# Sliding-window attention with a SwiGLU block: another order of attention among the feed-forward steps, turned q and k evicted from two banks, and another opening order

## The chip, the cores and the metric

The kernel runs on one core of a Trainium2 chip. The metric is the device time of one execution in microseconds (us). The kernel before has a median of 349.18 us over three runs (349.02 to 349.81). The profile is of one execution of its own. Matrix products run on TensorE (PE), which writes into PSUM, a memory of eight banks. VectorE (DVE) and ScalarE (ACT) read PSUM. GpSimd (POOL) works between tiles in SBUF. SyncE (SP) issues all DMA transfers in one queue.

## The reference

Attention has batch 8, 8 heads, 576 positions and head size 64. Each query sees itself and the 63 keys before it. The result is laid out as 4608 tokens of 512 values, and goes through a gated feed-forward block.

```python
scores = np.matmul(q, k.transpose(0, 1, 3, 2)) / np.sqrt(64)
mask = (rel >= 0) & (rel < 64)            # rel: query position minus key position
attn = softmax(np.where(mask, scores, -1e9))
x = np.matmul(attn, v).transpose(0, 2, 1, 3).reshape(4608, 512)
g = x @ w_gate                            # 512 x 1536
out = (g / (1 + np.exp(-g)) * (x @ w_val)) @ w_out    # w_out: 1536 x 512
```

## The kernel before, in words

Tokens are handled in three sizes. A *group* g is 128 tokens (36 of them), a *block* n is 256 tokens (18), and a *tile* t is 512 tokens (9). The weights stay in SBUF as bf16 after a load and a cast in six slices of 256 columns each (`weights`, `cast_w`; `weights_o`, `casts_o` for w_out). Step m of a tile uses slice m // 2 of both w_gate and w_val.

The attention part of a block loads q and k as f32 (`load`, `load1`, lines 77 to 93) and casts them to bf16 (`cast_k`). It then turns them so that the head dimension lies on the partitions. `turn2` (line 134) does this with eight TensorE transposes into one PSUM bank and copies that evict it. `turn1` (line 126) does it with transposing DMAs. v is loaded and cast per group, into one copy aligned with the group (`vo`) and one shifted by 64 tokens (`ve`).

For a group, `scores` (line 166) makes 16 small matmuls into two banks. `weigh` (line 180) takes the exponential on ScalarE and multiplies by the mask on VectorE (tile `E`, line 189). `products` (line 195) makes 16 small matmuls with v, whose last column of ones sums the weights, into two banks. `norm` (line 209) takes the reciprocal and multiplies, on VectorE, twice each. `turn_x` turns the result on TensorE and evicts it on ScalarE, while `turn_x1` (line 230) turns it by DMA, as in nearly all of the loop. Both write the tile's `xT`.

The feed-forward part of a tile has 12 steps. `step(t, m)` (line 260) makes four matmuls of 512 columns for g, four for v, and the tanh on ScalarE. It is put on a list. `finish()` (line 275) takes the oldest step from that list and does its two VectorE instructions, `sg` (line 278) and `hT` (line 279), which free the step's two banks. A step may cover a part of the 512 columns. `project(t, s)` (line 281) makes 12 matmuls for 128 tokens of a tile, an eviction on ScalarE and the output DMA.

PSUM is cut in two pools. Pool `ps_a` has four banks, given out in turn to turns, scores, products, projects and warm-up matmuls. Pool `ps_f` has two banks for g and two for v.

The order of the program is the order on every engine and in SP's queue. Nothing rearranges it; an instruction waits for its inputs and for its bank or buffer. The opening is a list written out by hand (lines 320 to 562). It runs attention for the first groups with `warm` matmuls (of zeros, line 293) in between, and then the 24 steps of tiles 0 and 1 and the four projects of tile 0, among the attention of groups up to 11. The loop (line 565) then takes one group number w at a time, from 8 to 35. It makes three steps of tile w // 4 and one project of the tile before. In an even w it makes the scores of groups w + 4 and w + 5, and in the odd one after it their products. Six steps and two projects with this attention work are called a *pair* below, and its steps the first to the sixth. In the kernel before, each finish comes one step after its step, and a project follows the third and the sixth step.

Of the kernel before, what the change touches and what calls it, by code (L numbers as in the profile page):

```python
# [8 lines left out]
P = 128  # L9
# [8 lines left out]
def kernel(  # L18
# [58 lines left out]
    def load(n, src, nm):  # L77

        x_f = stage.tile([P, H, 2, D], FP32, name=nm, tag=nm)
        for r, m, b, s, t in segments(256 * n, 256, 2):  # L80
            sp.dma_start(
                x_f[r:r + m].rearrange("r h c d -> r h (c d)"),
                src[b, :, s:s + t, :].rearrange("h (r c) d -> r h (c d)", c=2),
            )
        staged[nm, n] = x_f[:].rearrange("r h c d -> r c h d")
# [19 lines left out]
    def copy(eng, y, x):  # L105
        if eng is act:
            act.copy(y, x)  # L107
        else:
            eng.tensor_copy(y, x)  # L109
# [24 lines left out]
    def turn2(n, nm, eng):  # L134

        x_b = words.pop((nm, n))
        tp = ps_a.tile([P, 4, 2, P], BF16, name="tp", tag="a")
        for c in range(2):
            for p in range(4):
                nc.tensor.transpose(tp[:, p, c], x_b[:, c, P * p:P * p + P], identb[:])  # L140
        o = 64 if nm == "k_f" else 0
        ring = kT[n % KR] if nm == "k_f" else qT[n % QR]
        y = ring[:, :, o:o + 256].rearrange("r p (x c) -> r p x c", c=2)
        x = tp[:].rearrange("r p c x -> r p x c")
        if isinstance(eng, tuple):
            for i in range(2):
                copy(eng[i], y[:, 2 * i:2 * i + 2], x[:, 2 * i:2 * i + 2])
        else:
            copy(eng, y, x)

    def cast_v(g, engs):

# [100 lines left out]
    def casts_o(s, eng):  # L253
        copy(eng, wo[:, 2 * s:2 * s + 2, :], raw.pop((2, s))[:])
# [36 lines left out]
        sp.dma_start(out[n0:n0 + P, :], os_[:])  # L291

    def warm(n):
        w_ps = ps_a.tile([P, 512], FP32, name="w_ps", tag="a")
        for _ in range(n):
            nc.tensor.matmul(w_ps[:], wz[:, 0:P], wz[:])

# [20 lines left out]
            dve.memset(masks[i][0:64, i - 1, :], 0.0)  # L318

    begin()  # L320
    load(1, k, "k_f")
    load(0, q, "q_f")
    load(0, k, "k_f")
    load(1, q, "q_f")
    cast_k(0, "k_f", (act, pool))
    cast_k(0, "q_f", dve)
    warm(11)
    turn2(0, "q_f", (dve, act))
    load_vg(0)
    cast_v(0, pool)  # L330
    load_vg(2)
    cast_v(2, pool)
    cast_k(1, "k_f", (dve, act))
    warm(3)
    turn2(0, "k_f", (dve, act))
    load_vg(1)
    cast_k(1, "q_f", dve)
    turn2(1, "k_f", (dve, act))
    keys_before(1)
    warm(1)  # L340
    turn2(1, "q_f", (dve, act))
    scores(1)
    weigh(1)
    load(2, q, "q_f")
    warm(1)
    scores(0)
    weigh(0)
    warm(1)
    scores(2)
    weigh(2)  # L350
    cast_v(1, pool)
    cast_k(2, "q_f", (dve, act))
    load(3, k, "k_f")
    warm(5)
    products(0)
    norm(0)
    load(2, k, "k_f")
    scores(3)
    weigh(3)
    cast_k(3, "k_f", act)  # L360
    warm(2)
    turn2(2, "q_f", act)
    products(1)
    norm(1)
    turn_x(0)
    load_vg(3)
    cast_k(2, "k_f", (dve, pool))
    load(3, q, "q_f")
    warm(2)
    products(2)  # L370
    norm(2)
    warm(1)
    turn2(2, "k_f", dve)
    turn2(3, "k_f", act)
    weights(0, 1)
    weights(0, 0)
    cast_v(3, pool)
    load_vg(4)
    weights(3, 0)
    turn_x(1)  # L380
    cast_w(0, 0, pool)
    keys_before(3)
    weights(3, 1)
    load_vg(5)
    cast_k(3, "q_f", dve)
    warm(1)
    products(3)
    norm(3)
    keys_before(2)
    turn_x(2)  # L390
    cast_w(0, 1, dve)
    load_vg(6)
    turn2(3, "q_f", (dve, act))
    weights(4, 0)
    warm(1)
    turn_x(3)
    scores(5)
    weigh(5)
    scores(4)
    weigh(4)  # L400
    scores(6)
    weigh(6)
    cast_v(4, pool)
    weights(4, 1)
    cast_w(3, 0, pool)
    step(0, 1)
    step(0, 0)
    finish()
    load_vg(7)
    weights(5, 0)  # L410
    cast_w(3, 1, act)
    products(4)
    norm(4)
    step(0, 7)
    finish()
    weights(5, 1)
    weights(2, 0)
    cast_v(5, pool)
    cast_w(4, 0, pool)
    cast_v(6, act)  # L420
    turn_x(4)
    cast_w(4, 1, pool)
    products(5)
    norm(5)
    weights(2, 1)
    step(0, 6)
    finish()
    products(6)
    norm(6)
    scores(7)  # L430
    weigh(7)
    load_vg(8)
    step(0, 9)
    finish()
    turn_x(5)
    weights(1, 1)
    cast_v(7, pool)
    weights(1, 0)
    turn_x(6)
    cast_w(5, 1, pool)  # L440
    cast_w(5, 0, act)
    load_vg(9)
    load(4, k, "k_f")
    load(5, k, "k_f")
    step(0, 8)
    finish()
    products(7)
    norm(7)
    step(0, 11)
    finish()  # L450
    turn_x(7)
    load(5, q, "q_f")
    step(0, 10)
    finish()
    cast_w(2, 1, dve)
    cast_w(2, 0, act)
    step(1, 8)
    finish()
    load(4, q, "q_f")
    weights_o(2)  # L460
    step(0, 5)
    finish()
    step(0, 4, 0, 256)
    finish()
    load_vg(10)
    weights_o(1)
    cast_w(1, 0, dve)
    step(1, 7)
    finish()
    cast_v(9, pool)  # L470
    weights_o(3)
    cast_w(1, 1, dve)
    step(1, 4)
    finish()
    load_vg(11)
    keys_before(4)
    cast_k(4, "k_f", pool)
    step(1, 11)
    finish()
    step(1, 2)  # L480
    finish()
    cast_k(5, "k_f", (dve, pool))
    turn2(4, "k_f", act)
    weights_o(4)
    weights_o(5)
    step(0, 3)
    finish()
    step(1, 9)
    finish()
    cast_k(4, "q_f", (dve, pool))  # L490
    weights_o(0)
    casts_o(2, pool)
    cast_k(5, "q_f", (dve, pool))
    load1(6, k, "k_f")
    step(0, 2)
    finish()
    cast_v(8, pool)
    turn2(4, "q_f", (dve, act))
    step(0, 4, 256, 256)
    finish()  # L500
    scores(8)
    weigh(8)
    scores(9)
    weigh(9)
    step(1, 5)
    finish()
    products(8)
    norm(8)
    turn2(5, "q_f", act)
    keys_before(5)  # L510
    turn2(5, "k_f", act)
    load1(6, q, "q_f")
    step(1, 1)
    finish()
    products(9)
    norm(9)
    turn_x(8)
    casts_o(3, pool)
    step(1, 0)
    finish()  # L520
    casts_o(1, act)
    casts_o(5, dve)
    casts_o(4, dve)
    cast_k(6, "k_f", dve)
    casts_o(0, act)
    cast_v(11, pool)
    cast_v(10, dve)
    keys_before(6)
    cast_k(6, "q_f", (dve, pool))
    load(7, k, "k_f")  # L530
    scores(10)
    weigh(10)
    turn1(6, "k_f")
    turn1(6, "q_f")
    load_vg(12)
    scores(11)
    weigh(11)
    step(1, 10)
    finish()
    project(0, 3)  # L540
    project(0, 2)
    products(10)
    norm(10)
    turn_x1(9)
    project(0, 1)
    products(11)
    norm(11)
    load_vg(13)
    load1(8, k, "k_f")
    step(1, 3)  # L550
    finish()
    cast_k(7, "k_f", dve)
    step(1, 6)
    finish()
    turn_x(10)
    turn_x(11)
    load1(7, q, "q_f")
    load_vg(14)
    turn2(7, "k_f", dve)
    cast_v(12, pool)  # L560
    keys_before(7)
    project(0, 0)


    for w in range(8, NG):
        t, s = divmod(w, 4)
        n, odd = w // 2, w % 2
        step(t, 3 * s)
        finish()
        if odd:  # L570
            for g in (w + 3, w + 4):
                if g < NG:
                    products(g)
        if odd and n + 4 < NB:
            cast_k(n + 4, "k_f", pool)
        if not odd and n + 3 < NB:
            cast_k(n + 3, "q_f", pool)
        if w + 5 < NG:
            cast_v(w + 5, pool)
        step(t, 3 * s + 1)  # L580
        finish()
        if odd:
            for g in (w + 3, w + 4):
                if g < NG:
                    norm(g)
                    turn_x1(g)
        if not odd and w + 5 < NG:
            scores(w + 4)
            scores(w + 5)
            weigh(w + 4)  # L590
        step(t, 3 * s + 2)
        finish()
        if not odd and w + 5 < NG:
            weigh(w + 5)
        if odd and n + 4 < NB:
            turn1(n + 4, "k_f")
            keys_before(n + 4)
        if not odd and n + 3 < NB:
            turn1(n + 3, "q_f")
        project(t - 1, s)  # L600
        if odd and n + 5 < NB:
            load1(n + 5, k, "k_f")
        if w + 7 < NG:
            load_vg(w + 7)
        if not odd and n + 4 < NB:
            load1(n + 4, q, "q_f")
    finish()
    for s in range(4):
        project(8, s)
# [32 lines left out]
```

## Time and profile before

| what | value |
|---|---|
| median of three runs | 349.18 us |
| the profiled execution | 349.27 us |
| its span, first to last instruction | 347.6 us |
| TensorE busy | 330.8 us, 95% of the span |
| VectorE busy | 239.0 us, 69% |
| ScalarE busy | 146.9 us, 42% |
| GpSimd busy | 99.9 us, 29% |
| DMA queue, share of 16 engines | 76.2%, 56.51 MB |
| chain that ended last | PE 76%, DVE 11%, DMA 7%, issue 2%, ACT 2% |
| mean granted TensorE clock | 0.989 |

The profile's page counts busy time by engine, then cuts the span in 40 slices and gives the busy share of each in tenths. The chain is the work that ended last, followed back from the end: at each step to what released an instruction, or to the instruction before it on its engine. The lists of groups and waits name an instruction by line, engine and tile. "A <- B" in a wait says that A's engine stood idle until B was done. Matmuls overlap in the pipeline, so that four of 512 columns take 0.86 us from start to start of the next four, though each is shown as longer.

### The profile page before, as it was taken

How to read it: one execution, taken by the hardware profiler on the slowest of the kernel's cores; microseconds unless marked ns; L12 is line 12 of the kernel's file. 1: busy time of each engine (PE TensorE's matmuls, PEld its weight loads, DVE VectorE, ACT ScalarE, POOL GpSimd, SP SyncE). 2: the span in 40 equal slices, each digit the busy share in tenths (PEclk: the TensorE clock that was granted, in tenths of full speed). 3: DMA queues.
4: the chain of work that ended last, by engine and by line, in shares of the span. 5: the costliest groups of instructions: out<-in, count | busy, mean ns of one | idle time of the engine just before them, and what ended most of it. 6: DMA issues, size and time to landing. Idle time of an engine off the chain costs nothing.

```text
span 347.6 us, 6974 instructions
## 1 busy us (share of the span) xinstructions
PE 330.8 (95%) x2633; PEld 159.2 (46%) x2633; DVE 239.0 (69%) x500; ACT 146.9 (42%) x252; POOL 99.9 (29%) x145
## 2 busy tenths in 40 slices
PE   6787999999999999999999999989999999999995
PEld 2554444554544444444444444434444444444442
DVE  3788999998869676766676677667766666655510
ACT  1756763484352525252525252525252525223221
POOL 1635704710254242323323332324243220000000
PEclk9889999999999999999999999999999999999999
DMA  8999999995978989979798888988889331210012
GB/s 216 242 281 250 335 260 246 321 209 68 234 145 166 168 179 156 181 168 168 162 162 188 156 167 157 192 146 159 168 180 170 93 91 39 70 46 32 30 62 91
DMA packets 150834, 56.96 MB, mean 164 GB/s; under 512 B 125200, under 2 KB 144656, under 8 KB 150800
## 3 DMA queue, kind: packets, MB, share of 16 engines
q1 hardware_dynamic: 150800, 56.51, 76.2%
q8 instruction: 21, 0.34, 0.4%
q14 instruction: 13, 0.11, 0.1%
HBM read 37.75 MB, written 9.44 MB: 136 GB/s over the span
## 4 chain that ended last, share of the span: by engine, by line
PE 76%; DVE 11%; DMA 7%; issue 2%; ACT 2%; SPq 0%; DVEq 0%; ACTq 0%
PE o_ps L284 24%; PE g_ps L267 23%; PE v_ps L267 22%; DMA xT<-x_b 4%; DVE x_b L214 3%; DVE E L189 3%; PE ao_ps L203 2%; PE s_ps L174 2%; DMA k_f<-in_k_dram 2%; DVE sg L278 2%; PE tp L140 1%; DVE hT L279 1%; DVE r L213 1%; DVE q_fb L109 1%; DMA out_dram<-os__2927 1%
## 5 line engine op out<-in xcount | busy, mean ns | idle before, releaser
L267 PE MATMUL g_ps<-xT,wg 128*128 128x512 bf16 (+1 forms) x436 | 111.4, 378 | 4.2 <-DMA xT<-x_b 2.9
L267 PE MATMUL v_ps<-xT,wv 128*128 128x512 bf16 (+1 forms) x436 | 111.0, 377 | 0.0
L278 DVE SCALAR_TENSOR_TENSOR sg<-th,g_ps 128x512 f32<-128x512 f32 (+1 forms) x109 | 73.8, 677 | 47.5 <-ACT th L272 47.5
L272 ACT ACTIVATE th<-g_ps 128x512 f32<-128x512 f32 (+1 forms) x109 | 64.8, 595 | 86.3 <-PE g_ps L267 80.7
L284 PE MATMUL o_ps<-wo,hT 128*128 128x512 bf16 x432 | 98.3, 379 | 0.0
L279 DVE TENSOR_TENSOR hT<-sg,v_ps 128x512 bf16<-128x512 f32 (+1 forms) x109 | 74.4, 683 | 11.4 <-PE ao_ps L203 0.5
L267 PEld LDWEIGHTS <-wv 128*128 128x128 bf16 x436 | 42.7, 98 | 50.7
L284 PEld LDWEIGHTS <-hT 128*128 128x128 bf16 x432 | 42.2, 98 | 50.5
L267 PEld LDWEIGHTS <-wg 128*128 128x128 bf16 x436 | 39.4, 98 | 48.9 <-DMA xT<-x_b 4.2
L189 DVE TENSOR_TENSOR E<-E,mask 128x512 bf16<-128x512 bf16 x72 | 37.2, 550 | 21.2 <-ACT E L188 20.5
L109 POOL CAST ve<-v_f 64x512 bf16<-64x512 f32 x68 | 42.7, 628 | 4.2
L188 ACT ACTIVATE E<-s_ps 128x512 bf16<-128x512 f32 x72 | 38.4, 604 | 8.9 <-PE s_ps L174 8.7
L109 POOL CAST q_fb<-q_f 128x1024 bf16<-128x1024 f32 (+1 forms) x14 | 13.3, 952 | 77.6 <-DMA q_f<-in_q_dram 63.1
L109 POOL CAST vo<-v_f 128x512 bf16<-128x512 f32 x34 | 22.5, 663 | 36.7 <-DMA v_f<-in_v_dram 36.4
L214 DVE TENSOR_TENSOR x_b<-ao_ps,r 128x256 bf16<-128x256 f32 x72 | 30.6, 425 | 2.5
L109 POOL CAST k_fb<-k_f 128x1024 bf16<-128x1024 f32 (+1 forms) x14 | 13.8, 989 | 58.4 <-DMA k_f<-in_k_dram 53.9
L203 PEld LDWEIGHTS <-E 128*64 128x64 bf16 x576 | 11.5, 111 | 10.8 <-ACT th L272 5.5
L174 PE MATMUL s_ps<-qT,kT 64*128 64x64 bf16 x576 | 13.0, 191 | 3.0 <-ACT qT L107 2.2
L203 PE MATMUL ao_ps<-ve,E 128*64 128x65 bf16 x288 | 14.4, 197 | 0.9 <-DVE E L189 0.5
L213 DVE RECIPROCAL r<-ao_ps 128x4 f32<-128x4 f32 x72 | 12.5, 174 | 3.8 <-PE ao_ps L203 3.7
L174 PEld LDWEIGHTS <-kT 64*128 64x128 bf16 x576 | 10.2, 95 | 10.3 <-issue 8.8
L203 PE MATMUL ao_ps<-vo,E 128*64 128x65 bf16 x288 | 14.4, 198 | 0.0
(84 smaller groups left out, 121.8 us busy)
## 6 DMA issues: line engine op xcount, KB each, us to landing
v_f<-in_v_dram SPq DMA_DIRECT2D x32, 256.0 KB, 4.7
q_f<-in_q_dram SPq DMA_DIRECT2D x23, 256.0 KB, 5.2
k_f<-in_k_dram SPq DMA_DIRECT2D x21, 256.0 KB, 4.1
w_f<-in_moe_w_val_dram SPq DMA_DIRECT2D x6, 512.0 KB, 8.0
w_f<-in_moe_w_gate_dram SPq DMA_DIRECT2D x6, 512.0 KB, 7.7
wo_f<-in_moe_w_out_dram SPq DMA_DIRECT2D x6, 512.0 KB, 8.0
k_f<-in_k_dram SPq DMA_DIRECT2D x5, 512.0 KB, 6.5
q_f<-in_q_dram SPq DMA_DIRECT2D x4, 512.0 KB, 7.8
```

The lines of the kernel that those rows point to most:

```text
L109: eng.tensor_copy(y, x)
L174: nc.tensor.matmul(ps[a][:, p, b], kT[g // 2 % KR][y, p, o:o + P], qT[g // 2 % QR][y, p, o:o + 64], tile_position=(64 * a, 0),)
L188: act.activation(e, x[:], AF.Exp, scale=0.125)
L189: dve.tensor_mul(e, e, mk[:].unsqueeze(1).to_broadcast([P, 4, 2, 64]))
L203: nc.tensor.matmul(o_ps[64 * b:64 * b + 64, i, :], Es[g % ER][:, y, b], z[g % VR][:, y, :], tile_position=(0, 64 * b),)
L213: dve.reciprocal(r[:], o_ps[:, :, D])
L214: dve.tensor_mul(xb[g][:, 256 * h:256 * h + 256].rearrange("r (y d) -> r y d", y=4), o_ps[:, :, 0:D], r[:].unsqueeze(2).to_broadcast([P, 4 ...
L267: nc.tensor.matmul(ps[:, 0:n], w[:, c, P * m:P * m + P], xT[t][:, c, c0:c0 + n], start=(c == 0), stop=(c == 3),)
L272: act.activation(th[:, 0:n], g_ps[:, 0:n], AF.Tanh, scale=0.5)
L278: dve.scalar_tensor_tensor(sg[:, 0:n], th[:, 0:n], 1.0, g_ps[:, 0:n], ALU.add, ALU.mult)
L279: dve.tensor_mul(hT[t][:, m, c0:c0 + n], sg[:, 0:n], v_ps[:, 0:n])
L284: nc.tensor.matmul(o_ps[:], hT[t][:, c, P * s:P * s + P], wo[:, c, :], start=(c == 0), stop=(c == 11),)
```

## The change

There are four parts.

- `turn2` with two engines makes two tiles in two banks, each of half the rows, with all transposes ahead of the two copies. Before, both copies read one bank.
- `warm` takes its bank from the feed-forward pool.
- The opening list is in another order. It begins with k and q of block 0 and ends with turns of block 6 on TensorE, where the list before turned block 6 by DMA and k of block 7 on TensorE. Other engines do some of the casts. The first steps use weight slice 3, then 2, 1, 5, 4 and 0. The step that is cut is (1,7), in three parts (256, 128 and 128 columns) in place of (0,4) in two. The four projects come in the order 1, 0, 3, 2.
- The loop handles two groups at once, with the same steps and projects. The scores come after the first step of a pair, and the first project lies between the second and the third. The products come after the third step, and the second project between the fifth and the sixth. Each finish but the sixth's is put before the next step, some of them behind other work.

The diff follows. In the opening, removed lines are left out, as they are printed above.

```diff
@@ -134,19 +134,21 @@
     def turn2(n, nm, eng):
 
         x_b = words.pop((nm, n))
-        tp = ps_a.tile([P, 4, 2, P], BF16, name="tp", tag="a")
-        for c in range(2):
-            for p in range(4):
-                nc.tensor.transpose(tp[:, p, c], x_b[:, c, P * p:P * p + P], identb[:])
         o = 64 if nm == "k_f" else 0
         ring = kT[n % KR] if nm == "k_f" else qT[n % QR]
-        y = ring[:, :, o:o + 256].rearrange("r p (x c) -> r p x c", c=2)
-        x = tp[:].rearrange("r p c x -> r p x c")
-        if isinstance(eng, tuple):
-            for i in range(2):
-                copy(eng[i], y[:, 2 * i:2 * i + 2], x[:, 2 * i:2 * i + 2])
-        else:
-            copy(eng, y, x)
+        engs = eng if isinstance(eng, tuple) else (eng,)
+        m = 4 // len(engs)
+        tps = []
+        for i in range(len(engs)):
+            tp = ps_a.tile([P, m, 2, P], BF16, name="tp", tag="a")
+            for c in range(2):
+                for p in range(m):
+                    a = P * (m * i + p)
+                    nc.tensor.transpose(tp[:, p, c], x_b[:, c, a:a + P], identb[:])
+            tps.append(tp)
+        for i, tp in enumerate(tps):
+            y = ring[:, m * i:m * i + m, o:o + 256].rearrange("r p (x c) -> r p x c", c=2)
+            copy(engs[i], y, tp[:].rearrange("r p c x -> r p x c"))
 
     def cast_v(g, engs):
 
@@ -291,7 +293,7 @@
         sp.dma_start(out[n0:n0 + P, :], os_[:])
 
     def warm(n):
-        w_ps = ps_a.tile([P, 512], FP32, name="w_ps", tag="a")
+        w_ps = ps_f.tile([P, 512], FP32, name="w_ps", tag="g")
         for _ in range(n):
             nc.tensor.matmul(w_ps[:], wz[:, 0:P], wz[:])
 
@@ -318,292 +320,305 @@
...
             dve.memset(masks[i][0:64, i - 1, :], 0.0)
     begin()
+    load(0, k, "k_f")
+    load(0, q, "q_f")
+    cast_k(0, "k_f", (dve, act))
+    cast_k(0, "q_f", (act, pool))
+    warm(11)
+    turn2(0, "k_f", act)
+    load_vg(0)
     load(1, k, "k_f")
+    warm(3)
+    turn2(0, "q_f", dve)
+    warm(4)
+    scores(0)
+    cast_v(0, (pool, act, dve))
+    cast_k(1, "k_f", pool)
     load(1, q, "q_f")
+    scores(1)
     load_vg(2)
+    load(2, k, "k_f")
+    keys_before(1)
+    weigh(0)
+    cast_k(1, "q_f", dve)
+    weigh(1)
+    warm(2)
+    turn2(1, "k_f", act)
+    warm(2)
+    turn2(1, "q_f", (dve, act))
     load_vg(1)
     load(2, q, "q_f")
     products(0)
     norm(0)
     scores(3)
+    cast_k(2, "k_f", (dve, pool))
     weigh(3)
+    warm(1)
+    turn_x(0)
+    scores(2)
+    cast_v(1, (pool, None, None))
+    weigh(2)
+    load_vg(3)
+    turn2(2, "k_f", act)
+    load(3, k, "k_f")
+    cast_k(2, "q_f", (act, pool))
+    cast_v(2, (pool, dve, act))
+    cast_v(3, (act, pool, pool))
     warm(2)
     products(1)
     norm(1)
+    keys_before(2)
+    warm(4)
+    turn2(2, "q_f", (dve, act))
+    products(2)
     load(3, q, "q_f")
+    warm(1)
+    scores(5)
+    load_vg(4)
     norm(2)
     products(3)
     norm(3)
+    cast_k(3, "k_f", pool)
+    weigh(5)
+    turn_x(1)
+    scores(4)
+    weights(3, 0)
+    cast_k(3, "q_f", pool)
+    weigh(4)
     turn_x(2)
+    cast_v(4, (pool, None, None))
+    cast_w(3, 0, pool)
+    turn2(3, "k_f", act)
+    turn_x(3)
+    keys_before(3)
     warm(1)
+    turn2(3, "q_f", (act, dve))
+    weights(3, 1)
+    warm(2)
     products(4)
     norm(4)
+    cast_w(3, 1, dve)
+    scores(6)
+    load_vg(5)
+    weigh(6)
+    weights(2, 0)
     step(0, 7)
+    cast_v(5, (act, pool, pool))
+    scores(7)
+    finish()
+    weights(2, 1)
+    weigh(7)
+    cast_w(2, 0, act)
+    cast_w(2, 1, pool)
+    load_vg(6)
+    products(5)
+    load_vg(7)
+    step(0, 6)
+    turn_x(4)
+    norm(5)
+    cast_v(6, (act, pool, pool))
+    finish()
+    step(0, 5)
+    turn_x(5)
+    finish()
+    weights(1, 0)
+    cast_v(7, (pool, pool, act))
+    weights(1, 1)
+    cast_w(1, 0, pool)
+    products(6)
+    step(0, 4)
+    weights(5, 0)
     weights(5, 1)
+    products(7)
+    cast_w(1, 1, pool)
+    cast_w(5, 0, pool)
+    step(1, 7, 0, 256)
+    norm(6)
+    weights(4, 1)
+    load(4, q, "q_f")
+    finish()
+    turn_x(6)
+    weights(4, 0)
+    load(4, k, "k_f")
+    load(5, q, "q_f")
+    weights_o(1)
+    load_vg(8)
+    step(0, 3)
+    finish()
+    cast_w(5, 1, pool)
+    norm(7)
+    step(0, 2)
+    finish()
+    finish()
+    turn_x(7)
+    step(0, 10)
+    load_vg(9)
+    step(1, 10)
+    finish()
+    cast_k(4, "q_f", pool)
+    step(0, 11)
+    load(5, k, "k_f")
     cast_w(4, 1, pool)
+    cast_k(4, "k_f", pool)
+    cast_w(4, 0, act)
+    finish()
+    weights(0, 0)
+    load_vg(10)
+    keys_before(4)
+    weights(0, 1)
+    finish()
+    weights_o(0)
+    step(1, 2)
+    finish()
+    step(1, 9)
+    finish()
+    turn2(4, "q_f", (act, dve))
     step(0, 9)
+    turn2(4, "k_f", act)
+    casts_o(1, pool)
+    step(1, 6)
+    finish()
+    finish()
+    weights_o(3)
+    step(1, 7, 256, 128)
+    finish()
+    cast_k(5, "q_f", pool)
+    scores(9)
+    scores(8)
+    cast_v(8, (act, pool, pool))
+    weigh(9)
+    cast_w(0, 0, pool)
+    weights_o(2)
+    weights_o(5)
+    step(1, 11)
+    keys_before(5)
+    cast_k(5, "k_f", act)
     step(0, 8)
+    cast_v(9, (pool, dve, act))
+    finish()
+    finish()
+    weights_o(4)
+    cast_w(0, 1, pool)
+    load_vg(11)
+    weigh(8)
+    step(1, 3)
+    turn2(5, "q_f", act)
     step(1, 8)
+    products(8)
+    finish()
+    products(9)
+    finish()
+    norm(8)
+    step(0, 0)
+    casts_o(0, pool)
+    finish()
+    step(1, 1)
+    turn2(5, "k_f", act)
+    casts_o(3, pool)
+    norm(9)
+    load(6, k, "k_f")
+    turn_x(8)
+    load(6, q, "q_f")
+    step(0, 1)
+    finish()
+    scores(10)
+    cast_v(10, pool)
+    scores(11)
+    finish()
+    weigh(10)
+    load1(7, k, "k_f")
+    casts_o(5, pool)
+    casts_o(2, pool)
+    step(1, 0)
+    weigh(11)
+    casts_o(4, pool)
+    project(0, 1)
+    load_vg(12)
+    cast_v(11, (dve, None, None))
     step(1, 4)
     products(10)
+    cast_k(6, "q_f", pool)
+    finish()
+    cast_k(6, "k_f", (act, pool))
+    products(11)
+    turn_x1(9)
+    step(1, 7, 384, 128)
     norm(10)
+    project(0, 0)
     norm(11)
+    finish()
     load1(7, q, "q_f")
     load_vg(14)
+    turn2(6, "k_f", dve)
+    load1(8, k, "k_f")
+    load_vg(13)
+    project(0, 3)
+    step(1, 5)
+    keys_before(6)
+    turn_x(10)
     keys_before(7)
-    for w in range(8, NG):
+    turn2(6, "q_f", dve)
+    cast_k(7, "k_f", (dve, pool))
+    turn1(7, "k_f")
+    turn_x(11)
+    finish()
+    project(0, 2)
+    cast_v(12, (dve, act, act))
+    for w in range(8, NG, 2):
         t, s = divmod(w, 4)
-        n, odd = w // 2, w % 2
+        n = w // 2
         step(t, 3 * s)
         finish()
-        if odd:
-            for g in (w + 3, w + 4):
-                if g < NG:
-                    products(g)
-        if odd and n + 4 < NB:
-            cast_k(n + 4, "k_f", pool)
-        if not odd and n + 3 < NB:
+        if n + 3 < NB:
             cast_k(n + 3, "q_f", pool)
         if w + 5 < NG:
             cast_v(w + 5, pool)
+            scores(w + 4)
+            scores(w + 5)
+        finish()
+        if w + 5 < NG:
+            weigh(w + 4)
+        step(t, 3 * s + 1)
+        if w + 5 < NG:
+            weigh(w + 5)
+        finish()
+        if n + 3 < NB:
+            turn1(n + 3, "q_f")
+        project(t - 1, s)
+        if w + 7 < NG:
+            load_vg(w + 7)
+        if n + 4 < NB:
+            load1(n + 4, q, "q_f")
+        step(t, 3 * s + 2)
+        w, s = w + 1, s + 1
+        if w + 4 < NG:
+            products(w + 3)
+            products(w + 4)
+        finish()
+        step(t, 3 * s)
+        if w + 4 < NG:
+            for g in (w + 3, w + 4):
+                norm(g)
+                turn_x1(g)
+        if n + 4 < NB:
+            cast_k(n + 4, "k_f", pool)
+        if w + 5 < NG:
+            cast_v(w + 5, pool)
+        finish()
         step(t, 3 * s + 1)
         finish()
-        if odd:
-            for g in (w + 3, w + 4):
-                if g < NG:
-                    norm(g)
-                    turn_x1(g)
-        if not odd and w + 5 < NG:
-            scores(w + 4)
-            scores(w + 5)
-            weigh(w + 4)
-        step(t, 3 * s + 2)
-        finish()
-        if not odd and w + 5 < NG:
-            weigh(w + 5)
-        if odd and n + 4 < NB:
+        if n + 4 < NB:
             turn1(n + 4, "k_f")
             keys_before(n + 4)
-        if not odd and n + 3 < NB:
-            turn1(n + 3, "q_f")
         project(t - 1, s)
-        if odd and n + 5 < NB:
+        if n + 5 < NB:
             load1(n + 5, k, "k_f")
         if w + 7 < NG:
             load_vg(w + 7)
-        if not odd and n + 4 < NB:
-            load1(n + 4, q, "q_f")
+        step(t, 3 * s + 2)
     finish()
     for s in range(4):
         project(8, s)
```

## The prediction, made before the changed kernel had run

> **What bounds the kernel now.** I read the busy rows by slice first, then a table by stage, then the chain that ended last, then the waits of TensorE in the loop. The profiled execution took 349.27 us, of which 347.6 us is the span. The page's slices (40 of 8.7 us):
>
> ```profile
> PE   6787999999999999999999999989999999999995
> DVE  3788999998869676766676677667766666655510
> PEclk9889999999999999999999999999999999999999
> ```
>
> TensorE is full from slice 5 on, with small dents; VectorE is full in slices 4 to 8. The table by stage, cut where the stages change:
>
> ```profile
> 6.70:20.00 13.30, 9.44 (x125) 5.97 (x126) 10.14 (x20) 8.59 (x16) 6.43 (x10) 0.85 1.27 248
> 20.00:31.60 11.60, 8.96 (x152) 5.94 (x150) 8.33 (x23) 6.40 (x12) 5.28 (x8) 0.88 1.17 288
> 31.60:44.10 12.50, 11.28 (x121) 5.76 (x118) 12.09 (x27) 9.87 (x19) 8.58 (x11) 1.00 1.04 301
> 44.10:95.10 51.00, 50.61 (x409) 25.79 (x409) 45.72 (x91) 26.12 (x43) 13.73 (x19) 1.00 0.95 222
> 95.10:347.60 252.50, 245.79 (x1825) 114.25 (x1822) 160.77 (x323) 94.61 (x165) 64.63 (x90) 1.00 0.67 134
> ```
>
> Columns are PE, PEld, DVE, ACT, POOL busy, clock, DMA share, GB/s. The first feed-forward step starts at 31.57. From there to 44.1 VectorE is busy 12.09 of 12.50 us; from 44.1 to 95.1, where the loop starts, TensorE lacks 0.4 us. The chain confirms who rules the opening:
>
> ```profile
> 30.74 4.08 DVE E L189 x6
> 34.82 0.61 DVE sg L278
> ...
> 42.14 1.29 DVE E L189 x2
> 43.44 0.61 DVE sg L278
> 44.04 0.04 issue
> 44.09 1.02 PE g_ps L267 x4
> ```
>
> VectorE's queue carries the end until 44.09, when step (0,8) gets its bank; TensorE carries it afterwards. In the loop TensorE waits for one thing only (waits, then its timeline at the worst place):
>
> ```profile
> PE g_ps L267 <- DMA xT<-x_b: 2.9, 4, 1.2
> ```
> ```profile
> 227.60 1.03 PE L267 MATMUL g_ps<-xT,wg 128*128 128x512 bf16 x4
> 228.47 1.03 PE L267 MATMUL v_ps<-xT,wv 128*128 128x512 bf16 x4
> 229.33 2.75 PE L284 MATMUL o_ps<-wo,hT 128*128 128x512 bf16 x12
> 233.25 1.02 PE L267 MATMUL g_ps<-xT,wg 128*128 128x512 bf16 x4 [1.17 <-DMA xT<-x_b]
> ```
>
> A project keeps TensorE for 2.59 us, so the step should start near 231.9 and starts at 233.25. From one even project to the next the chain gives 16.97 us where nothing waits (100.97, 117.94, 134.90) and 17.53, 17.65, 18.29, 17.97 around the four waits: 0.56 + 0.68 + 1.32 + 1.00 = 3.56 us. A step costs 1.73 us (g 0.865, v 0.865).
>
> **The change, part by part.**
>
> *Loop.* A project now lies between steps, products come before the pair's fourth step instead of after it, and a sixth step follows the odd project. From products to the first step of the next tile stood 2 steps + a project = 6.05 us; now 3 steps + a project, 7.78 us: 1.73 us more for norm, transposing DMA and landing. What starts them doesn't move: in both, one step and the products lie between the end of the even project and norm, the output write and loads of v and q stand ahead of the transposes in SP's queue, and norm waits for one finish. So the landings should keep their distance from the project. In the wait at 163.38 that is 163.25 - 154.47 = 8.8 us, needed at 10.15 now; at the worst place 0.4 us stays. Gain 3.56 us, between 2.5 (landing a us later) and 3.56.
>
> What waits newly here: finish of the fourth step stands behind two norms (2.27 us from 157.39 to 159.66). They begin about 1.5 us after the third step, so that finish ends at 1.5 + 2.27 + 1.4 = 5.2 us; the sixth step, which takes its banks, starts at 0.64 + 1.73 + 1.73 + 2.59 = 6.7. Price 0, with 1.5 us of cover. Scores ahead of the second step put two exponentials (1.2 us) in front of its tanh on ScalarE; its finish is needed after a project and a step, 4.3 us later. Price 0. The last finish, which project (7,3) used to cover, has 11 matmuls of project (8,0), 2.38 us, against about 1.5: 0, at most 0.3.
>
> *Split evictions.* Before, two engines took halves of one bank, and ScalarE's half waited for VectorE's (ACT qT <- DVE qT 4.2 us in 3 waits). In the changed order ScalarE's half waits for TensorE alone. That saves up to 0.7 us of latency on each split turn; it takes no work from VectorE (0.69 us a half), so I count it only in the walk below. The second bank of the four is paid by later tiles; warm gives its bank back, as it now uses a feed-forward one.
>
> *Opening.* First the loads. In the opening DMA is never idle, and landings follow bytes: k 0 (1.57 MB issued by then) at 8.48, k 2 (4.46 MB) at 20.64, gate block 0 (6.29 MB) at 28.39. That is 2.0 us + bytes / 0.24 MB/us. Two weight blocks by the waits at 37.58 and 41.78 (9.17 and 10.5 MB) give 0.315 afterwards. In the new order: k 0 at 4.2, q 0 6.4, k 1 9.6, q 1 11.8, k 2 15.1, q 2 18.4, k 3 21.7, q 3 23.8, v 4 24.9, blocks 3 (6.55 MB) between 28.2 and 29.2, blocks 2 at 32 to 34, blocks 1 at 37 to 39, blocks 5 at 41 to 43.
>
> Then the engines in their new order. q 2 at 18.4, its cast, 8 transposes and two evictions end at 21.9; scores (5) follow, and from there VectorE's queue has no gap that I find. Its work after 21.9: norm 2 and 3 (2.27, and 0.4 waiting for products 3), weigh 5 and 4 (2.56, at 0.64 an E), the small v copies and keys 0.63, half a q turn 0.69, norm 4 1.13, the cast of value block 3 0.69, weigh 6 1.28: 31.6. That cast waits for the load, with weigh 6 and the first finish behind it; VectorE arrives at 29.5, the block by 29.2, so nothing is added if the rate holds, and each us of lateness beyond is a us of everything. The first step runs at 29.4 to 31.1. Then finish 1.37, weigh 7 1.28, norm 5 1.13, two finishes 2.75, norm 6 1.13, finish 1.37, the part step 0.83, norm 7 1.13, two finishes 2.75: 45.3. TensorE follows it, waiting for banks twice, and at 45.4 has done 7.5 steps, products up to 7 and turn_x up to 7. The kernel before has 6 steps and products 7 at 46.28. The difference: 0.88 + 1.5 x 1.73 + 0.24 for the turn = 3.7 us.
>
> Here a rule speaks against the change, since it leaves more casts to GpSimd beside VectorE's weighing. The row: E takes 412 ns at least, 780 at the median before 44.1 (up to 1251), 424 at the median in the loop. The Trainium skill (SBUF — State Buffer, "Who interferes with whom") says that a VectorE instruction with two SBUF inputs contends with a GpSimd one that reads SBUF, and that the later one is blocked whole. By it each E meeting a 1.04 us cast could wait for half of it, about 0.95 us each, an estimate; the 8 E of my sum would be 2.5 us later. In the chain, 14 E take 9.01 us, 0.64 each, beside 11.7 us of GpSimd work from 6.7 to 31.6; the new order has 9.9 before the first step. I take 0.64 and keep 2.5 for the range.
>
> What takes some back: six turns on TensorE after the first step instead of five (0.45 us; in return two fewer transposing DMAs on SP), the third part of the cut step 0.1. Handing-over: the chain up to 46 us has 2.8% "issue", 1.3 us, and my walk has none; half for half the stretch, and a little for weights that come late after 45.4 (before lacks 0.4 there): 0.9. Of the blocks after 45.4, blocks 0 should land near 60 and are used near 66, the output weights near 69 and from 74. Warm matmuls are 33 instead of 29, in idle time. Net gain 3.7 - 0.45 - 0.1 - 0.9 = 2.2 us, between -0.4 (E blocked whole) and 3.2.
>
> Sum: 349.27 - 3.56 - 2.2 = 343.5 us for an execution like the profiled one. The median of the runs, 349.18, is 0.09 lower, so 343.4.
>
> **Rivals.**
>
> *Only the loop gains* (0.20). E is blocked as the rule says, or VectorE's backlog is only moved: at the first step it still holds weigh 6 and 7 and norms 5 to 7. Then the opening yields -0.5 to 1: 345 to 346. For it: VectorE has the same masks, norms and finishes in both. Against: behind its first step stood 9.6 us of weighing and norms (four of each), and 6.0 now (two and three).
>
> *The opening gains more* (0.14). DMA runs at 0.30 MB/us early, as it does from 31.6 to 44.1, the turns' latency falls fully, and step one comes by 28: 4 to 5 us, 340.5 to 341.8. For it: ScalarE's 18.5 us and GpSimd's 9.9 before the first step leave room. Against: VectorE's sum above.
>
> *Slower* (0.05, and 0.03 for no change). Finish behind the norms holds the banks: the sixth step waits in each of the 13 pairs. It decides from 1.5 us of delay on; to undo 5.8 us it takes 0.45 us more, about 2 us in each pair, giving 349.5 or later. For it: VectorE has 9.3 of 10 us in the slice of 240 to 250. Against: norms read PSUM and kept 2.27 us beside GpSimd's casts.
>
> That the split doesn't part the engines is excluded by the changed wait.
>
> **How the numbers follow.** My forecast, both gains: 0.58, 342.2 to 344.8, likeliest 343.4. The range reaches into the case with the loop alone and into that with the larger opening: 340.9 to 346.2. Faster by over 0.2% (0.7 us, about what a measurement of this kernel can tell from no change): 0.92; within: 0.03; slower: 0.05.
>
> **What would show it.** The xT waits are gone from TensorE's list and every pair takes 16.97 us; if they remain with smaller numbers, landings moved. The first step starts at 29 to 30.5; the loop at 92.0 to 93.5 (95.1 before). VectorE is full from 22 to 45, with E near 0.64. ScalarE's qT no longer waits for VectorE's. Wrong would be: a new wait of g_ps for VectorE in each pair; the cast of block 3 waiting past 30; starts of E beyond 0.9 us; idle TensorE between 50 and 90.

## The result, and the profile after

The changed kernel takes 343.94 us (median of four runs, 343.48 to 344.15) against 349.10 us before. The ratio is 0.9846, with a 95% interval of 0.9829 to 0.9863. The profiled execution took 344.15 us, the longest of the four, with a span of 342.4 us (347.6 before). These are the rows of the page that answer to those of before, in slices of 8.6 us:

```profile
PE   7667999999999999999999999999999999999995
DVE  3869887988587676767676867666776766655510
PEclk9988999999999999999999999999999999999999
```

The one dent that TensorE's row had in the loop before (the 8 in its 27th slice, around the wait that ends at 233.25) is gone. The opening is still four slices long. The table by stage (PE, PEld, DVE, ACT, POOL busy, clock, DMA share, GB/s), cut at the first step and at the start of the loop:

```profile
6.70:20.00 13.30, 8.32 (x145) 5.05 (x147) 10.13 (x23) 9.27 (x15) 3.87 (x5) 1.00 1.25 238
20.00:31.40 11.40, 7.26 (x136) 5.46 (x138) 9.03 (x25) 7.38 (x13) 6.50 (x8) 0.85 1.02 272
31.40:45.40 14.00, 13.54 (x126) 7.20 (x128) 12.83 (x29) 9.68 (x17) 9.52 (x11) 0.88 1.06 284
45.40:93.80 48.40, 48.09 (x394) 25.06 (x399) 38.88 (x78) 26.29 (x44) 19.38 (x23) 1.00 1.03 234
93.80:342.40 248.60, 243.55 (x1797) 114.52 (x1822) 162.72 (x324) 95.51 (x167) 62.83 (x89) 1.00 0.69 136
```

The loop starts at 93.8 instead of 95.1, which is 1.3 us. From there to the end it takes 248.6 us instead of 252.5, which is 3.9 us. The first step is hardly earlier (31.4 against 31.57). The chain shows what carried the opening:

```profile
12.80 8.04 DMA q_f<-in_q_dram
...
25.90 2.59 DVE E L191 x4
28.52 1.01 DVE ve L162
29.54 0.03 issue
29.57 0.29 DVE ve L162
...
31.43 1.34 PE g_ps L269 x4
32.77 1.28 PE v_ps L269 x3
```

The load of q for block 2 lands at 20.84, and VectorE leads to the first step from there on. One of its two small v copies takes 1.01 us, the other 0.29. The first step runs at about half the clock (1.34 us for four matmuls that take 0.86 later; the granted clock is 0.50 from 31.9 to 35.3).

In the loop no matmul waits for another engine or for a transfer: the list of such waits, which had xT in it before, is empty. At a tile's edge its timeline and SP's show the room that is left:

```profile
191.12 2.75 PE L286 MATMUL o_ps<-wo,hT 128*128 128x512 bf16 x12
193.71 1.03 PE L269 MATMUL g_ps<-xT,wg 128*128 128x512 bf16 x4
194.57 1.03 PE L269 MATMUL v_ps<-xT,wv 128*128 128x512 bf16 x4
195.43 0.81 PE L269 MATMUL g_ps<-xT,wg 128*128 128x512 bf16 x3
```
```profile
186.01 0.35 SPq L293 DMA_DIRECT2D out_dram<-os__2941  x1
186.41 0.43 SPq L101 DMA_DIRECT2D v_f<-in_v_dram  x1
186.90 1.59 SPq L92 DMA_DIRECT2D q_f<-in_q_dram  x2
189.49 3.14 SPq L237 DMA_TRANSPOSE xT<-x_b  x2
```

The two transposes are issued 4.1 us after the even project's end (185.36), as before (193.09 after 188.96). The next tile's first step is the one at 195.43, so they have 5.9 us. In the kernel before they had 4.2 us (from 193.09 to 197.3, which is 2.59 us after the start of the odd project at 194.72), and the step came at 197.99.

### The profile page after: what moved, and what is told of

It reads as the page before. It is cut to its first block, busy times and chain, and to the rows that moved or that the text cites. A ratio compares the mean times of both kernels' runs of the same rounds, so it can differ in the third digit from the quotient of the medians.

```text
span 342.4 us, 6997 instructions
## 1 busy us (share of the span) xinstructions
PE 326.2 (95%) x2612; PEld 159.3 (47%) x2653; DVE 236.0 (69%) x496; ACT 150.0 (44%) x258; POOL 103.4 (30%) x143
## 4 chain that ended last, share of the span: by engine, by line
PE 90%; DMA 4%; DVE 2%; SPq 1%; ACT 1%; issue 1%; ACTq 0%
PE g_ps L269 28%; PE o_ps L286 27%; PE v_ps L269 27%; DMA q_f<-in_q_dram 4%; PE ao_ps L205 3%; PE s_ps L176 3%; PE tp L147 1%; SPq L81 1%; DVE E L191 1%; PE xtp L229 0%; DVE ve L162 0%; ACT q_fb L107 0%; SPq L101 0%; ACT kT L107 0%; DVE x_b L216 0%
## 5 line engine op out<-in xcount | busy, mean ns | idle before, releaser
L280 DVE SCALAR_TENSOR_TENSOR sg<-th,g_ps 128x512 f32<-128x512 f32 (+2 forms) x110 | 74.0, 673 | 57.1 <-ACT th L274 56.7
L269 PE MATMUL v_ps<-xT,wv 128*128 128x512 bf16 (+2 forms) x435 | 111.0, 377 | 0.1
L274 ACT ACTIVATE th<-g_ps 128x512 f32<-128x512 f32 (+2 forms) x110 | 64.8, 589 | 78.9 <-PE g_ps L269 76.1
L281 DVE TENSOR_TENSOR hT<-sg,v_ps 128x512 bf16<-128x512 f32 (+2 forms) x110 | 74.5, 677 | 11.3
L109 POOL CAST q_fb<-q_f 128x1024 bf16<-128x1024 f32 (+1 forms) x17 | 17.0, 1002 | 85.5 <-DMA q_f<-in_q_dram 84.2
L191 DVE TENSOR_TENSOR E<-E,mask 128x512 bf16<-128x512 bf16 x72 | 34.7, 510 | 9.5 <-ACT E L190 8.6
L109 POOL CAST ve<-v_f 64x512 bf16<-64x512 f32 x57 | 35.9, 630 | 5.8 <-DMA v_f<-in_v_dram 2.4
L109 POOL CAST k_fb<-k_f 128x1024 bf16<-128x1024 f32 (+1 forms) x16 | 15.7, 981 | 55.9 <-DMA k_f<-in_k_dram 50.0
L109 POOL CAST vo<-v_f 128x512 bf16<-128x512 f32 x30 | 19.0, 633 | 15.4 <-DMA v_f<-in_v_dram 15.0
```

The lines of the kernel that those rows point to most:

```text
L191: dve.tensor_mul(e, e, mk[:].unsqueeze(1).to_broadcast([P, 4, 2, 64]))
L269: nc.tensor.matmul(ps[:, 0:n], w[:, c, P * m:P * m + P], xT[t][:, c, c0:c0 + n], start=(c == 0), stop=(c == 3),)
L274: act.activation(th[:, 0:n], g_ps[:, 0:n], AF.Tanh, scale=0.5)
L280: dve.scalar_tensor_tensor(sg[:, 0:n], th[:, 0:n], 1.0, g_ps[:, 0:n], ALU.add, ALU.mult)
L281: dve.tensor_mul(hT[t][:, m, c0:c0 + n], sg[:, 0:n], v_ps[:, 0:n])
```

## The experiments

All times are medians. "Before" was measured anew beside each group of runs, at 349.2 to 349.5 us, and each ratio is against it.

**1 and 2. The loop and the opening by themselves.** e1_new_loop_only is the kernel before with the loop of the changed one. e2_new_opening_only is the changed kernel with the loop of before.

> The old opening and old turns with the new loop. By my theory the loop's gain is the four waits for xT (3.56 us) and does not depend on the opening: 349.1 - 3.6 = 345.5 us, no wait of g_ps for a DMA left, the loop starting at 95.1 as before. Rival: part of the loop's gain (the profile shows 3.7 to 3.9 between loop start and end) comes from what the new opening leaves behind (loads ahead, banks free): then less than 3 us, 346.1 or more, with xT waits left in the first tiles.

> The new opening and split turns with the old loop. By my theory the opening gives the 1.3 us that its loop start shows (93.8 against 95.1), and the four waits come back in full: 349.1 - 1.3 = 347.8 us. Rival: the waits depend on how the loop is entered; then the sum of this gain and that of the new loop alone differs from 5.2 us by more than 0.7.

The new loop alone gives 346.27 us (0.9911, 0.989 to 0.9933): 3.0 us, and none of its matmuls waits for a DMA in the loop. The new opening alone gives 345.13 us (0.9876, 0.985 to 0.9902): 4.1 us. Together they give 5.2 and not 7.1. By the second expectation this speaks for its rival: what the waits cost depends on the execution and on how the loop is entered. e2 ran from 344.15 to 347.56 us. Its profiled execution, the longest, still has the waits:

```profile
PEld L269 <- DMA xT<-x_b: 3.5, 3, 1.4
PE g_ps L269 <- DMA xT<-x_b: 1.8, 2, 1.0
```

By the times of its even projects that execution lost 2.6 us to them. None of e2's short executions was profiled, so the share that the new opening saves by weakening the waits stays open. Seen the other way, the opening is worth 2.3 us where the loop is new (346.27 to 343.94), and the loop 1.2 us where the opening is new.

**3. Products moved back.**

```diff
         w, s = w + 1, s + 1
+        finish()
+        step(t, 3 * s)
         if w + 4 < NG:
             products(w + 3)
             products(w + 4)
         finish()
-        step(t, 3 * s)
...
-        finish()
         step(t, 3 * s + 1)
         finish()
```

> The changed kernel, with only the products of a pair moved back behind the fourth step; scores, projects and finishes of the others stay. My theory: the time from products to the next tile's first step is 6.05 us again instead of 7.78, so the xT waits return, 3.0 to 3.6 us together: 347.0 to 347.6. Rival: it is the project between the steps that removes the waits, since it keeps TensorE busy while the transposes land; then the time stays within 0.5 us of 343.9.

It took 343.95 us (0.9842, 0.9819 to 0.9865), so the theory that the waits need this room to go fails. The transposes have 4.2 us from issue (190.32) to need (194.54), as little as in the kernel before, and yet there is no wait. They land sooner. SP's list, for all loop transposes of the kernel before, of the changed one and of this one, min, median and max:

```profile
DMA to landing us min/median/max: 2.4/2.8/4.7
```
```profile
DMA to landing us min/median/max: 2.4/2.9/5.3
```
```profile
DMA to landing us min/median/max: 2.4/2.4/3.9
```

**4 and 5. One step moved alone, in the loop of before.** e5_project_early puts the even project, with its output write and loads, ahead of the third step. e6_products_early puts products ahead of the fourth step, and norm and the transposes ahead of the fifth.

```diff
-        step(t, 3 * s + 2)
-        finish()
-        if not odd and w + 5 < NG:
-            weigh(w + 5)
+        if odd:
+            step(t, 3 * s + 2)
+            finish()
...
         project(t - 1, s)
...
+        if not odd:
+            step(t, 3 * s + 2)
+            finish()
+            if w + 5 < NG:
+                weigh(w + 5)
```
```diff
+        if odd:
+            for g in (w + 3, w + 4):
+                if g < NG:
+                    products(g)
         step(t, 3 * s)
         finish()
         if odd:
             for g in (w + 3, w + 4):
                 if g < NG:
-                    products(g)
+                    norm(g)
+                    turn_x1(g)
...
-        if odd:
-            for g in (w + 3, w + 4):
-                if g < NG:
-                    norm(g)
-                    turn_x1(g)
```

> The kernel before, with only the even project of a pair, its output write and the loads behind it moved ahead of the third step; products stay behind the fourth. Theory that the products' place took the waits away (the prediction's): products still lie 6.69 us ahead of the next tile, so the waits stay, within 0.7 us of 349.2. Theory formed after the products were moved back without harm: the output write and the loads of v and q run 1.73 us earlier than the transposes, which then land in 2.4 us rather than 2.8 or more; the waits vanish, 346.0 to 346.7 us.

> The kernel before, with only the products moved ahead of the fourth step, and norm and the transposes ahead of the fifth; project and loads stay. The prediction's theory: 1.73 us more until the next tile, waits gone, 345.7 to 346.5 us. Theory of the loads: the transposes now come straight behind the loads in the queue and land later, so most of the waits stay: 347.5 or more.

Both are slower than before: 360.5 us (1.0313, 1.0291 to 1.0336) and 353.23 us (1.0106, 1.0087 to 1.0124). Neither theory had foreseen that. The waits of TensorE in the loop of e5:

```profile
PE o_ps L284 <- ACT E L188: 5.4, 12, 0.4
PE g_ps L267 <- DMA xT<-x_b: 3.4, 3, 1.3
PE g_ps L267 <- DVE sg L278: 1.8, 3, 0.9
PE g_ps L267 <- DVE hT L279: 1.3, 1, 1.3
```

The project now follows the scores at once and waits in each pair until an exponential has read its bank. The second group's weighing falls behind the tanh of a third step that comes later, and with it the finishes and norm. So at a tile's edge the transposes start too late: at the step of 167.72 they are issued at 163.77, 2.8 us before they are needed (166.55). They do land in 2.4 us at the median, as the second theory said. All but one of the waits in the last three rows, one of 0.2 us, are at the first step of a tile.

In e6, products follow the project at once and wait for its eviction. Norm ends earlier, but the transposes stand in SP's queue behind the output write and the loads:

```profile
157.90 0.37 SPq L291 DMA_DIRECT2D out_dram<-os__2439  x1
158.31 0.43 SPq L101 DMA_DIRECT2D v_f<-in_v_dram  x1
158.78 2.28 SPq L92 DMA_DIRECT2D q_f<-in_q_dram  x3
161.17 2.97 SPq L235 DMA_TRANSPOSE xT<-x_b  x2
```

Norm was done at 159.8, and the issue came 1.4 us after it. They land in 3.4 us at the median, and three waits for xT remain (1.4 us). A pair takes 17.33 us instead of 16.96 (even projects at 137.32 and 154.65). The changed loop avoids both, as its scores come one step earlier and a step lies between scores and project, and between project and products.

**6. The loads behind the transposes,** in the kernel before, with TensorE's order untouched:

```diff
                     norm(g)
                     turn_x1(g)
+            if w + 6 < NG:
+                load_vg(w + 6)
+            if n + 4 < NB:
+                load1(n + 4, q, "q_f")
...
-        if w + 7 < NG:
+        if odd and w + 7 < NG:
             load_vg(w + 7)
-        if not odd and n + 4 < NB:
-            load1(n + 4, q, "q_f")
```

> The kernel before, with only the loads of v and q that follow the even project moved behind the two transposes of the pair, so that these no longer run among 0.77 MB of loads. Order of TensorE's work is untouched: the transposes still have about 4.4 us from issue to need. Theory that the loads make them late: they land in 2.4 us each, the waits go: 345.7 to 346.7. Theory that only more time before the next tile helps (the prediction's): waits stay, 348.8 or more. A possible cost: q and v land 4 us later, so GpSimd's casts, and with them products, may come late.

It took 346.35 us (0.9917, 0.9892 to 0.9942), as little as with the whole new loop (346.27). The transposes are issued 4.1 us after the even project's end, as before (192.11 after 187.97), and have 4.2 us until they are needed, as before. But they land in 2.4 us at the median and 3.6 at most:

```profile
DMA to landing us min/median/max: 2.4/2.4/3.6
```

No matmul waits for xT (one weight load does, for 0.2 us). So it was the loads among the transposes that made them late. More time and fewer loads are two ways to the same gain.

**7 and 8. The split evictions.** e4_one_bank is the changed kernel with the old `turn2`. e7_split_only is the kernel before with the new `turn2` and with `warm` on a feed-forward bank.

```diff
-        engs = eng if isinstance(eng, tuple) else (eng,)
-        m = 4 // len(engs)
-        tps = []
-        for i in range(len(engs)):
-            tp = ps_a.tile([P, m, 2, P], BF16, name="tp", tag="a")
...
+        tp = ps_a.tile([P, 4, 2, P], BF16, name="tp", tag="a")
...
+        if isinstance(eng, tuple):
+            for i in range(2):
+                copy(eng[i], y[:, 2 * i:2 * i + 2], x[:, 2 * i:2 * i + 2])
```

The diff is that of e4. For `turn2`, e7's is its reverse.

> The changed kernel with the old turn of q and k: both engines evict halves of one bank, one after the other. Three turns before the first step are split (q of blocks 1, 2 and 3), and one after it. My theory: the split saves latency of 0.6 to 0.7 us on each, of which that of block 2 lies on the chain (its load is waited for, and scores 5 wait for both halves): 0.5 to 1.0 us slower, 344.4 to 344.9. Rival: the split does nothing for the time, as the two copies' latency hides behind other work: within 0.3 us of 343.9. Or it costs by the second bank: 0.5 us faster.

> The kernel before, with only the split turns and warm on a feed-forward bank. Six turns up to (3, q) and (4, q) are split. Theory from the one-bank run (0.8 us faster without the split): a split turn holds two of four banks, and products or scores wait for one of them: between no change and 1 us slower, 349.2 to 350.2. The prediction's theory: up to 0.7 us saved per turn on the chain of the opening, 1 us or more faster: 348.2 or less.

Without the split the changed kernel takes 343.10 us (0.982, 0.9795 to 0.9845). In the old opening the split and the bank of `warm` together take it to 347.82 us (0.9943, 0.9921 to 0.9965), a gain of 1.6 us; no run parts the two. The first is against my theory, the second against the theory that I had formed from the first. The profile of the changed kernel has a wait that the one-bank run has not. The second half of products 4, at 30.77, waits for the bank of a turned q (block 3):

```profile
PE ao_ps L205 <- DVE qT L109: 0.9, 1, 0.9
```

But that is not the whole difference. In the one-bank run q 2 was cast at 20.54 and not at 20.94, and the two small v copies took 0.61 us and not 1.34. The copies led to the next runs.

**9 and 10. GpSimd's cast beside VectorE's copies, and the load of v 2.** e10_gate_cast_act moves one cast; e8_v2_later moves one load.

```diff
-    cast_w(3, 0, pool)
     turn2(3, "k_f", act)
...
     turn2(3, "q_f", (act, dve))
+    cast_w(3, 0, act)
```
```diff
     scores(1)
-    load_vg(2)
...
     load(2, q, "q_f")
+    load_vg(2)
```

> The changed kernel, with only the cast of gate block 3 moved from GpSimd to ScalarE, behind the turn of q for block 3. In the profile that cast (from 28.35) runs just ahead of VectorE's two copies of v for group 4 (from 28.52), which take 1.34 us; in two variants where VectorE comes first they take 0.61. Theory of the shared port: the copies take 0.61 and the first step comes up to 0.7 us earlier: 343.1 to 343.5. Rival: the copies are slow for another reason or off the chain: 343.7 to 344.1. The 0.8 us of the one-bank run would then be the bank's.

> The changed kernel, with the load of v for group 2 behind the load of q for block 2 (it is cast after that q anyway). Theory: the opening hangs on q of block 2, which lands at 20.84 us in the profile; 0.26 MB less ahead of it, at 0.21 to 0.24 MB/us, brings it 1.1 us earlier, and the first step with it: 342.8 to 343.3. Rival: VectorE's queue bounds the opening, not the load: no change, 343.7 to 344.1; or v of group 2 itself then comes last, no change or slower.

e10 took 342.21 us (0.9794, 0.9769 to 0.982), the best of all. Its timeline and that of the changed kernel, around the copies:

```profile
27.80 0.61 DVE L162 COPY ve<-vo 64x520 bf16<-64x520 bf16 x2 [0.51 <-POOL vo L109]
28.53 1.12 ACT L107 CAST wg<-w_f 128x1024 bf16<-128x1024 f32 x1
29.91 1.04 PE L269 MATMUL g_ps<-xT,wg 128*128 128x512 bf16 x4
```
```profile
28.35 1.04 POOL L109 CAST wg<-w_f 128x1024 bf16<-128x1024 f32 x1 [0.46 <-DMA w_f<-in_moe_w_gate_dram]
28.52 1.34 DVE L162 COPY ve<-vo 64x520 bf16<-64x520 bf16 x2
31.36 1.41 PE L269 MATMUL g_ps<-xT,wg 128*128 128x512 bf16 x4
```

In the changed kernel GpSimd's cast starts 0.17 us ahead of the copies, and the first copy lasts until the cast has ended. With the cast on ScalarE the copies take 0.61 us and the first step comes at 29.91. That is 1.45 us earlier; 0.73 of it is the copies, and 0.67 is q 2, which was cast at 20.27 in that execution and at 20.94 in the other. That cast of q lies ahead of the edit in the program, and whether the edit moves it is not shown. Another 0.5 us of the difference came after the first step (the loop's first project starts at 95.80 and at 97.78), where the clock was 1.00 and not 0.59.

e8 took 342.53 us (0.9802, 0.9782 to 0.9822). Its cast of q 2 starts at 17.70, 3.2 us earlier where I had expected 1.1, and its v copies take 0.61 us too. But GpSimd's cast then blocks the next copy in VectorE's queue, that of the keys, which takes 1.04 us and not 0.23. The first step comes at 30.66; then the value block is waited for. In the one-bank run it was the same, and the changed kernel's copy of the keys is shown behind it:

```profile
27.99 0.61 DVE L160 COPY ve<-vo 64x520 bf16<-64x520 bf16 x2 [0.51 <-POOL vo L109]
28.47 1.04 POOL L109 CAST wg<-w_f 128x1024 bf16<-128x1024 f32 x1 [0.51 <-DMA w_f<-in_moe_w_gate_dram]
28.64 0.96 DVE L124 COPY kT<-kT 128x256 bf16<-128x256 bf16 x1
```
```profile
29.89 0.23 DVE L124 COPY kT<-kT 128x256 bf16<-128x256 bf16 x1
```

From the first v copy to the end of the keys both take 1.6 us. So VectorE gains nothing when the v copies go first; the three runs with the cast on ScalarE (e10, e11 and e12) are the only ones of this opening in which no copy is blocked there. In the first 60 us of all 14 profiles, each copy of v or of keys that began during a GpSimd cast ended 0.07 to 0.19 us after that cast.

**11 and 12. Both together, with two banks and with one.**

> The load of v for group 2 behind q of block 2, and the cast of gate block 3 on ScalarE. If the two gains are apart: 1.4 + 0.5 below the changed kernel, 341.8 to 342.2. If the later load already let VectorE's copies go first (0.61 us in its profile), nothing is left for the cast: 342.3 to 342.7.

> As the run before it, with the old turn in one bank. If the one-bank gain of 0.8 us was only VectorE's copies going first, the bank is worth nothing here: within 0.4 us of the run before it. If the second bank costs by itself: 0.5 us or more faster than that run. If the split saves latency on the chain: slower by 0.5 us.

They took 342.43 us (0.981, 0.9784 to 0.9836) and 342.99 us (0.9819, 0.9789 to 0.9848). The two gains do not add up: with both edits the first step, at 29.66, waits for the weights (0.4 us for ScalarE's cast in e11's profile, which starts at 28.54 when the load has landed). One bank or two makes no difference beyond the intervals, and the 0.8 us of the one-bank run is not found again. The interval of that run overlaps the changed kernel's, and the copies going first don't explain it, so whether the 0.8 us are the bank's, the earlier q's or chance stays open.

## Why the prediction was right

*The loop, 3.56 us.* Right in size where the opening is the old one: 3.0 us by the loop alone (its interval is 2.3 to 3.8), every pair at 16.96 us, no wait for xT, transposes issued at the distance foretold. The new waits priced at zero (the finish behind two norms, the tanh behind exponentials, the last finish) do not show. Too narrow was the step "From products to the first step of the next tile ... 1.73 us more": this room is enough, but it isn't needed. Products moved back took nothing away. The transposes are then issued 1.8 us after the last load at the tile's edge near 190, where it was 1.0 us in the changed kernel and 0.9 before, and they land sooner. The prediction did not name the loads as the reason why they landed late, which moving them alone shows. Project and products had to move together: either alone, in the loop of before, made it 4 to 11 us slower, by other waits.

*That the two gains add up* did not hold. Alone they give 3.0 and 4.1 us, together 5.2. The parts of 3.56 and 2.2 are found only when the loop is counted first.

*The opening, 2.2 us.* Right as a sum: 2.3 us where the loop is new. In the profiled execution it is 1.3, with the loop's start at 93.8, just outside the forecast of 92.0 to 93.5. Terms failed inside. The first step came at 31.4 and not at 29.4, and at 45.4 TensorE had finished 5.5 steps and was in the next, where the walk had finished 7.5. That is some 3 us of steps:

- The landing rule of 2.0 us + bytes / 0.24 gave q 2 at 18.4, and it landed at 20.84: later transfers were already moving beside it, which the rule leaves out. Up to q 2, 3.93 MB had been issued, and 4.65 MB had moved when it landed (223 GB/s over 20.84 us).
- "The small v copies and keys 0.63" took 1.6, as the first copy stood behind GpSimd's cast.
- The clock fell. In 32 to 36 us it was 0.59 in this execution and 0.68 in e2's, but 1.00 in e3's with the same opening. In the 3.4 us ahead of the fall TensorE was busy for 1.45 us (28.49 to 31.90), and in e2 for 1.17 (27.70 to 31.10). In e3 and e10, where the clock stayed at 1.00, it was busy for 2.17 and 2.22 us there. I had not priced that, and where the border lies is not shown.

Against this, E took 0.65 in the chain as assumed, and at the median of 16 only 0.42 (0.78 before). After 45.4 TensorE lost no more than before (48.09 of 48.40 us are busy). At the loop's start the kernel was only 0.9 us behind the forecast's 92.9 (95.1 less 2.2). So the forecast had what lies behind 45.4 some 2 us too dear, in terms that nothing here separates. That the sum came out near is in part luck: errors of opposite sign.

*The rule on the shared port.* I took the row (0.64 an E) and left the rule's 2.5 us to the range. For E the row was right on average; single ones still took up to 1.26 us. But the rule's mechanism was there, on an instruction that I had priced at 0.2 us: a copy with one input. That is the other half of the Trainium skill's section ("Who interferes with whom", SBUF — State Buffer): copies and casts can take the shared pair, the later one is blocked for the whole instruction, and the order of issue decides. The traces agree: 0.29 us alone and 1.01 behind the cast for v, 0.23 and 0.96 to 1.04 for the keys.

*The split*, counted at nothing outside the walk: with the bank of `warm` it gave 1.6 us in the old opening, and it gives nothing measurable in the new one. As foretold, ScalarE's half of a turn of q no longer waits for VectorE's. Why the two openings differ is not shown; one candidate is the second bank, for which products 4 waited 0.9 us.

## What to carry to other kernels

When an engine waits for a transfer at a stage's edge, look at what else is in that queue at that moment, besides the order of the computing: moving two loads behind two transposes gained as much here as a new loop. A piece moved alone can lose what the pieces moved together gain, because banks and finishes follow; try the combination before giving up on the part. Where GpSimd and VectorE both work in SBUF on the chain to a first step, keep the large cast off GpSimd at that moment: moving that one line was worth 1.7 us here, of which the profile gives 0.7 to the copies. Letting the small copy go first doesn't do it, when the next small copy then meets the cast.

## What the runs showed of the hardware that was not expected

- A bf16 copy of 64x520 on VectorE takes 0.29 us, and 1.01 us if a GpSimd cast of 128x1024 has begun 0.17 us before it. A copy of the keys of 128x256 takes 0.23 us, and 0.96 to 1.04 behind such a cast. Which of the small copies meets the cast differs between executions of one opening: the first copy of v in the changed kernel and in e3, the second in e2.
- A transposing DMA of 128x512 lands 2.4 us after issue at the median with the loads behind it, and up to 4.7 to 5.6 us with some 0.8 MB of loads just ahead of it in the same queue.
- The granted clock fell to 0.50 for 3.4 us (31.9 to 35.3) after 3.4 us in which TensorE was busy for 1.45 us, though it idled for no longer than 1.3 us at a time.
